# A decode block with attention and MLP: the pieces of w2's last row over six DMA engines, the bias loaded once, and o turned earlier on TensorE

## Chip, core and metric

The kernel runs on one core of a Trainium2 chip. The metric is device time in microseconds; 721.72 us is the median of three runs before the change (721.49 to 721.81). The profile is of one further execution.

## What is computed

For two sequences with one new token each (B = 2, D = 576), a sigmoid gate mixes an attention block and an MLP, all in float32:

```python
g = sigmoid((x * gate_w).sum(-1, keepdims=True))
# A: 32 heads, 4096 cached keys and values per head, head size 128
q = (x @ wq)                                  # 576 x 4096
scores = einsum("bhqd,bhkd->bhqk", q, k_cache) * 128 ** -0.5
o = einsum("bhqk,bhkd->bhqd", softmax(scores), v_cache)
a = o @ wo                                    # 4096 x 576
# B: hidden size 4608
b = gelu_tanh(x @ w1 + b1) @ w2 + b2          # 576 x 4608, then 4608 x 576
out = g * a + (1 - g) * b
```

The two caches hold 268 MB, the weights 40 MB; each byte is used once.

## The kernel before

**Loads.** All large loads are issued by SyncE (SP) into one ring in SBUF with three slots of 128 x 16384 floats. The order is fixed by a list: wq, w1, then K and V of sixteen groups of four heads in turn, then three "last" loads. A load is issued when the load three places ahead of it has been used up (`load_next`). `LAST` says what is in the last three: w2 rows 0-27 (in the layout `(p r) n`, each of the 128 partitions holds 36 rows of w2, and a "row" r in this text is the r-th row of every partition); then w2 rows 28-35 with `wx` and the first rows of wo (32 such rows); then the rest of wo in ever smaller transfers. The page's queue q1 carries these loads, q10 the small ones that ScalarE (ACT) issues.

**The pieces `wx`.** The last 288 columns of w2's row 35 are not in the main transfer (L158) but are loaded separately (L155): 128 runs of 288 floats, in four DMAs, to 16 partitions. The outer dimension of each of the four DMAs has XE = 4 entries, one to a DMA engine, with XS = 8 runs each. Since these rows then lie in other partitions than their multipliers, `hg[:, NF - 1]` is spread by small matmuls with slices of the identity into `hx` (L411, L415), and `mlp_x` multiplies `hx` with the pieces.

**Attention.** For each of the sixteen groups: VectorE multiplies K with the spread-out q (L506), VectorE and GpSimd sum over the head size (L510 to L512), the maximum and the exponentials follow (L516 to L531), and TensorE multiplies with V (`av`, L545). `keep` and `combine` gather the results in `oall`.

**The end.** `acc` in PSUM sums the MLP's output and wo's first rows (`acc_mm`, L367: each row is two halves of 288 columns, four matmul instructions). `mlp_out(lo, hi)` does rows of w2, `wo_out(0, FOLD)` rows 0 to 22 of wo, `last_out` copies `acc` to SBUF (L446), folds it into `res` (L467) together with wo's rows 23 to 31 (L457, L481), copies `res` out and stores it. Before wo, the attention result must be normalised (`norm_sum`), transposed (`norm_t`) and turned (`o_turn`) into the layout of wo's rows, `oP`. The order on TensorE is the order of the program's text: rows 0-13 of w2, the last `av`, rows 14-17, `combine`, the sums, rows 18-27, `norm_t`, `mlp_x`, `o_turn`, rows 28-35, wo.

**The bias.** b1 is loaded by ACT's queue for both sequences into `b1r`, once in one DMA (L218, at the start) and once in five, and is added to the hidden layer's sums (L390); L395 to L405 compute the gelu, `hg`. The second K load waits for `hg`.

Of the kernel before, what the change touches and what calls it, by code (L numbers as in the profile page):

```python
# [8 lines left out]
F32 = mybir.dt.float32  # L9
# [3 lines left out]
P = 128  # L13
# [6 lines left out]
def kernel(  # L20
# [14 lines left out]
    nc = tc.nc  # L35
    B, H, SK, DH = k_cache.shape
    D = x.shape[-1]
# [12 lines left out]
    NG = 4  # L50
# [3 lines left out]
    F4 = F // NG  # L54
    FR = F4 // P
    FB = 3
    FC = F4 // FB
    NF = F // P
    NC = 4
    DO = D // NC  # L60
    NS = 2
    DS = D // NS
# [2 lines left out]

    LAST = (
        (("w2", 0, 14), ("w2", 14, 28)),
        (("w2", 28, 36), ("wx", 0, 1), ("wo", 0, 8), ("wo", 8, 16)),
        (("wo", 16, 23), ("wo", 23, 27), ("wo", 27, 30), ("wo", 30, 31), ("wo", 31, 32)),
    )  # L70
    FOLD = 23
    SLOT = R * DH
# [8 lines left out]
    cp = ctx.enter_context(tc.tile_pool(name="cp", bufs=1))  # L81
# [8 lines left out]
    ps_sm = ctx.enter_context(tc.tile_pool(name="ps_sm", bufs=3, space=bass.MemoryType.PSUM))  # L90
# [8 lines left out]
    kt, vt, wqt, w1t, rows = {}, {}, {}, {}, {}  # L99
# [22 lines left out]
    def slot(n):  # L122
        k = len(held) % SLOTS
        return ring[:, k * SLOT:k * SLOT + n]
# [7 lines left out]

    srcs = {"w2": w2.rearrange("(p r) n -> p (r n)", r=NF), "wo": wo.rearrange("(p r) n -> p (r n)", r=32)}

    XE, XC = 4, 4
    XP = XE * XC
    XS = P // XP
    srcx2 = w2.rearrange("(e c s r) n -> c r e s n", e=XE, c=XC, s=XS)[:, NF - 1, :, :, DS:]

    def length(w, a, z):  # L140
        return XS * DS if w == "wx" else (z - a) * D - (DS if (w, z) == ("w2", NF) else 0)

    def load_last(m):
        n = sum(length(*q) for q in LAST[m])

        used["e"], used["z"] = len(held) % SLOTS * SLOT + n, (len(held) % SLOTS + 1) * SLOT
        t = slot(n)
        o = 0
        for w, a, z in LAST[m]:
            if w == "wx":  # L150
                xt = t[:XP, o:o + XS * DS]
                rows[w] = xt.rearrange("p (s n) -> p s n", s=XS)
                o += XS * DS
                for c in range(XC):
                    nc.sync.dma_start(xt[c::XC].rearrange("e (s n) -> e s n", s=XS), srcx2[c])  # L155
                continue
            if (w, z) == ("w2", NF):
                nc.sync.dma_start(t[:, o:o + length(w, a, z)], srcs[w][:, a * D:z * D - DS])  # L158
                for r in range(a, z):
                    rows[w, r] = t[:, o + (r - a) * D:o + min((r - a + 1) * D, length(w, a, z))]  # L160
                o += length(w, a, z)
                continue

            ends = (a * D, a * D + DS, a * D + DS + DO, z * D) if (w, z) == ("wo", 32) else (a * D, z * D)
            for u, v in zip(ends, ends[1:]):
                nc.sync.dma_start(t[:, o:o + v - u], srcs[w][:, u:v])
                o += v - u
            for r in range(a, z):
                rows[w, r] = t[:, o - (z - r) * D:o - (z - r - 1) * D]

    def temp(n, parts=P):
        t = ring[:parts, used["t"]:used["t"] + n]
        used["t"] += n
        assert used["t"] <= SLOTS * SLOT
        return t

    def late(n, parts=P):
        t = ring[:parts, used["e"]:used["e"] + n]
        used["e"] += n
        assert not seq and used["e"] <= used["z"]  # L180
        return t

    def load():
        if not seq:
            return
        kind, i = seq.pop()
        if kind == "wq":
            wqt[i] = load_w(wq, ROWS[kind], i)
        elif kind == "w1":
            w1t[i] = load_w(w1, ROWS[kind], i)  # L190
        elif kind == "k":
            kt[i] = load_heads(k_cache, i)
        elif kind == "v":
            vt[i] = load_heads(v_cache, i)
        else:
            load_last(i)
        if kind in ("k", "v", "last"):
            held.append((kind, i))
# [9 lines left out]
    b1r = temp(F4)  # L208
# [3 lines left out]
    load()  # L212
    load()

    def load_b1(b, ends):
        to, src = b1r.rearrange("(g q) n -> g q n", g=NG)[:, b], b1.rearrange("(g n) -> g n", g=NG)
        for u, v in zip(ends, ends[1:]):
            nc.scalar.dma_start(to[:, u:v], src[:, u:v])  # L218


    load_b1(0, (0, F4))
    for b in range(B):
        nc.scalar.dma_start(xg[b:b + 1], x[b])
    nc.scalar.dma_start(xg[B:B + 1], gate_w[None, :])
# [4 lines left out]
    ident = cp.tile([P, P], F32, name="ident")  # L229
# [9 lines left out]
    for j in range(NPB):  # L239
        t = cp.tile([P, NT * 32 + EB], F32, name=f"p{j}")  # L240
# [71 lines left out]
    for m, ps in enumerate(qps):  # L312
        nc.scalar.copy(qrow[:, m * 512:(m + 1) * 512], ps)
    nc.scalar.dma_start(b2r, b2[None, :])
    load_b1(1, (0, 232, 464, 696, 928, F4))

    to = temp(HG * NO).rearrange("p (f o) -> p f o", f=HG)
# [7 lines left out]
    for f in range(HG):  # L327
# [7 lines left out]
    row4 = temp(E, NO)  # L335
    nc.vector.tensor_reduce(row4, ident[:NO, :NO].rearrange("p (i e) -> p e i", e=E), AX.X, ALU.add)
    spread = cp.tile([NO, P], F32, name="spread")
    nc.vector.tensor_copy(
        spread.rearrange("p (e c) -> p e c", e=E), row4.unsqueeze(2).to_broadcast([NO, E, PE_])
    )  # L340
    qs = {}
# [19 lines left out]
    acc = ps_acc.tile([P, DS], F32, name="acc")  # L361

    def acc_mm(lhsT, rhs, k, start=False, stop=False, lo=0):
        m = lhsT.shape[-1]
        for s in range(lo, lo + rhs.shape[-1] // DS):
            o = 64 * (k % 2) + 32 * s
            nc.tensor.matmul(  # L367
                acc[o:o + m], lhsT, rhs[:, (s - lo) * DS:(s - lo + 1) * DS], start=start, stop=stop, skip_group_check=True
            )

    g1z = cp.tile([1, 2, 32], F32, name="g1z")
    nc.gpsimd.memset(g1z, 0.0)
# [1 line left out]
    for k in range(2):  # L374
        acc_mm(g1z[:, k], b2r, k, start=True)
# [17 lines left out]

    ht = temp(F4).rearrange("p (r c) -> p r c", c=32)
    nc.vector.transpose(ht, hrow.rearrange("q (p r) -> q r p", r=NF))  # L395
    hb = ht[:, :, :B]
    hg = cp.tile([P, NF, B], F32, name="hg")
    t = temp(NF * B).rearrange("p (r b) -> p r b", b=B)
    nc.vector.tensor_mul(t, hb, hb)
# [6 lines left out]

    load()

    hxps = ps_sm.tile([XP, XS, B], F32, tag="sm", name="hxps")
    for s in range(XS):  # L410
        nc.tensor.matmul(  # L411
            hxps[:, s], ident.rearrange("p (q s) -> p s q", s=XS)[:, s], hg[:, NF - 1], start=True, stop=True
        )
    hx = cp.tile([XP, XS, B], F32, name="hx")
    nc.scalar.copy(hx, hxps)  # L415

    def mlp_x():
        for s in range(XS):
            acc_mm(hx[:, s], rows["wx"][:, s], s, lo=1)

    def mlp_out(lo, hi):
        for r in range(lo, hi):
            acc_mm(hg[:, r], rows["w2", r], r)
# [4 lines left out]
    oP = cp.tile([P, B, 32], F32, name="oP")  # L428

    def o_turn(turn):  # L430
        t = late(B * 32).rearrange("p (b c) -> p b c", c=32)
        for b in range(B):
            nc.vector.transpose(t[:, b], oT[:, b])
        ps = ps_sm.tile([P, B * 32], F32, tag="sm", name="op_t")
        nc.tensor.matmul(ps, turn, t.rearrange("p b c -> p (b c)"), start=True, stop=True)
        nc.vector.tensor_copy(oP.rearrange("p b c -> p (b c)"), ps)

    def wo_out(lo, hi):
        for r in range(lo, hi):
            acc_mm(oP[:, :, r], rows["wo", r], r)  # L440
# [127 lines left out]
    def norm_sum():  # L568
        sums = ps_sm.tile([NO, 1], F32, tag="sm", name="psum")
        nc.tensor.matmul(sums, rs, ones, start=True, stop=True)  # L570
        f = late(1, NO)
        nc.vector.reciprocal(f, sums)
        nc.vector.tensor_mul(f, f, gall)
        nc.vector.tensor_reduce(osum, oall.rearrange("p (r d) -> p d r", d=DH), AX.X, ALU.add)
        nc.vector.tensor_scalar_mul(osum, osum, f[:, 0:1])

    def norm_t():
        ps = ps_sm.tile([P, NO], F32, tag="sm", name="oT_t")
        nc.tensor.transpose(ps, osum, ident[:NO, :NO])
        nc.vector.tensor_copy(  # L580
            oT.rearrange("p b (h e) -> p h b e", e=E), ps.rearrange("p (h b e) -> p h b e", b=B, e=E)
        )

# [29 lines left out]
    turn = late(P)  # L613
    nc.scalar.copy(turn.rearrange("p (h k) -> p k h", k=KB), ident.rearrange("p (k h) -> p k h", k=KB))
    osum = late(DH, NO)
    norm_sum()
    mlp_out(18, 28)
    norm_t()
    mlp_x()
    o_turn(turn)  # L620
    mlp_out(28, NF)
    wo_out(0, FOLD)
    last_out()

# [27 lines left out]
```

## Time and profile before

| | |
|---|---|
| runs | 721.49, 721.81, 721.72 us; median 721.72 |
| the profiled execution's own time | 721.61 us |
| its span, first to last instruction | 719.7 us |
| mean granted TensorE clock | 0.658 |
| busy: DVE / PE / POOL / PEld / ACT | 71 / 30 / 20 / 9 / 6% of the span |
| DMA | 308.85 MB, mean 429 GB/s; queue q1 99.2% of 16 engines' span |
| last stretch | 310 GB/s in the last fortieth of the span, 417 to 449 in most of the others |

Shares are of the span. "DMA share" is the mean busy share of the sixteen DMA engines; it can come out a little over 1 in a short stretch. The granted clock is 1.00 at full and 0.50 at half speed of TensorE. The timeline's rows are start, duration, engine, line, operation, operands and count; in brackets stands the idle time of the engine before them and what ended it.

### The profile page before, as it was taken

How to read it: one execution, taken by the hardware profiler on the slowest of the kernel's cores; microseconds unless marked ns; L12 is line 12 of the kernel's file. 1: busy time of each engine (PE TensorE's matmuls, PEld its weight loads, DVE VectorE, ACT ScalarE, POOL GpSimd, SP SyncE). 2: the span in 40 equal slices, each digit the busy share in tenths (PEclk: the TensorE clock that was granted, in tenths of full speed). 3: DMA queues.
4: the chain of work that ended last, by engine and by line, in shares of the span. 5: the costliest groups of instructions: out<-in, count | busy, mean ns of one | idle time of the engine just before them, and what ended most of it. 6: DMA issues, size and time to landing. Idle time of an engine off the chain costs nothing.

```text
span 719.7 us, 3881 instructions
## 1 busy us (share of the span) xinstructions
PE 216.2 (30%) x1647; PEld 62.6 (9%) x1647; DVE 511.8 (71%) x136; ACT 40.0 (6%) x156; POOL 145.0 (20%) x35
## 2 busy tenths in 40 slices
PE   0665022040515050404032140505050503113195
PEld 0322000010101010101000010101010100000032
DVE  0004969779695969596969879696959695988910
ACT  0110010100001010101010100001010101010000
POOL 2000130404050403022040404040503122040400
PEclk9977556575756575566657575657575665757599
DMA  9999999999999999999999999999999999999997
GB/s 409 412 446 427 423 452 415 459 416 452 423 437 424 444 426 430 442 430 441 433 431 437 430 426 444 427 437 437 437 427 448 419 434 433 430 441 434 417 424 310
DMA packets 7278, 308.85 MB, mean 429 GB/s; under 512 B 830, under 2 KB 1362, under 8 KB 1628
## 3 DMA queue, kind: packets, MB, share of 16 engines
q1 hardware_dynamic: 7204, 308.55, 99.2%
q8 instruction: 13, 0.21, 0.1%
q10 hardware_dynamic: 56, 0.05, 0.0%
q14 instruction: 5, 0.04, 0.0%
HBM read 308.59 MB, written 0.00 MB: 429 GB/s over the span
## 4 chain that ended last, share of the span: by engine, by line
DMA 47%; DVE 35%; PE 15%; ACT 1%; issue 1%; ACTq 1%; POOL 0%; DVEq 0%; SPq 0%; POOLq 0%
DMA ring<-in_A_k_cache_dram 38%; DVE ring L506 19%; DVE s L511 10%; PE av L545 10%; DVE s L512 5%; DMA ring<-in_B_w_dram 4%; DMA ring<-in_A_wo_dram 3%; DMA ring<-in_gate_w_dram 3%; PE oall L562 2%; PE qps L303 2%; PE acc L367 1%; DVE avs L556 1%; ACTq L218 0%; PE qps L328 0%; ACT p L531 0%
## 5 line engine op out<-in xcount | busy, mean ns | idle before, releaser
L506 DVE TENSOR_TENSOR ring<-ring,q 128x16384 f32<-128x16384 f32 x16 | 275.6, 17225 | 109.1 <-DMA ring<-in_A_k_cache_dram 109.1
L510 POOL TENSOR_TENSOR ring<-ring 128x3968 f32<-128x3968 f32 x16 | 137.0, 8565 | 490.1 <-DVE ring L506 490.1
L545 PE MATMUL av<-ring,p 128*32 128x512 f32 x1024 | 137.5, 698 | 166.9 <-ACT p L531 166.9
L511 DVE TENSOR_REDUCE s<-ring 128x66 f32<-128x8448 f32 x16 | 143.3, 8953 | 1.3
L562 PE MATMUL oall<-avs,pick 128*64 128x512 f32 x16 | 14.8, 1028 | 196.7 <-DVE avs L556 168.3
L512 DVE TENSOR_REDUCE s<-ring 128x62 f32<-128x3968 f32 x16 | 68.4, 4277 | 0.1
L545 PEld LDWEIGHTS av<-ring,p 128*32 128x32 f32 x1024 | 35.1, 127 | 274.8 <-issue 217.8
L531 ACT ACTIVATE p<-s,bs 32x128 f32<-32x128 f32 x64 | 25.5, 398 | 478.9 <-DVE bs L525 477.7
L351 PE MATMUL qb<-qm,spread 64*128 64x512 f32 x8 | 8.3, 1138 | 72.5 <-POOL qm L347 72.5
L390 DVE TENSOR_TENSOR ring<-hps,ring 128x384 f32<-128x384 f32 x3 | 1.7, 559 | 33.3 <-PE hps L303 33.1
L562 PEld LDWEIGHTS oall<-avs,pick 128*64 128x64 f32 x16 | 2.2, 196 | 203.5 <-DVE avs L556 203.5
L367 PE MATMUL acc<-ring,hg 128*2 128x288 f32 x142 | 11.9, 487 | 26.1 <-DMA ring<-in_B_w_dram 26.1
L283 DVE TENSOR_SCALAR gb<-gb 128x2 f32<-128x2 f32 x1 | 0.2, 170 | 24.7 <-ACT gb L282 24.7
L556 DVE TENSOR_TENSOR avs<-av,selr 128x512 f32<-128x512 f32 x8 | 5.5, 682 | 10.6 <-PE av L545 10.6
L303 PE MATMUL hps<-ring 128*32 128x384 f32 x120 | 12.8, 598 | 0.0
L347 POOL TENSOR_TENSOR qm<-qall,mine 64x512 f32<-64x512 f32 x4 | 4.1, 1032 | 41.7 <-ACT qall L330 41.7
L477 DVE COPY ring<-res 2x144 f32<-2x144 f32 x1 | 0.3, 297 | 16.4 <-PE res L457 16.4
L531 ACT ACTIVATION_READ_ACCUMULATOR p<-s,bs 32x1 f32 x64 | 11.8, 184 | 0.0
L303 PE MATMUL qps<-ring 128*32 128x512 f32 x80 | 11.3, 729 | 0.0
L270 PE MATMUL xps<-ident,ring 3*128 3x3 f32 x10 | 1.5, 254 | 24.0 <-DMA ring<-in_gate_w_dram 23.1
L351 PEld LDWEIGHTS qb<-qm,spread 64*128 64x128 f32 x8 | 2.0, 307 | 75.6 <-POOL qm L347 75.6
L353 ACT COPY q<-qb 128x512 f32<-128x512 f32 x4 | 2.3, 586 | 106.3 <-PE qb L351 106.3
(87 smaller groups left out, 74.3 us busy)
## 6 DMA issues: line engine op xcount, KB each, us to landing
ring<-in_B_w_dram SPq DMA_DIRECT2D x2, 4608.0 KB, 34.4
ring<-in_B_w_dram SPq DMA_DIRECT2D x2, 4032.0 KB
ring<-in_A_wo_dram SPq DMA_DIRECT2D x2, 2304.0 KB, 14.9
ring<-in_B_w_dram SPq DMA_DIRECT2D x1, 2160.0 KB
ring<-in_A_wo_dram SPq DMA_DIRECT2D x1, 2016.0 KB
ring<-in_B_w_dram SPq DMA_DIRECT2D x1, 1152.0 KB, 14.7
ring<-in_A_wo_dram SPq DMA_DIRECT2D x1, 1152.0 KB
ring<-in_A_wq_dram SPq DMA_DIRECT2D x1, 1024.0 KB
```

The source lines that it names most:

```text
L303: nc.tensor.matmul(ps[32 * j:32 * j + 32, :width], lhs, ts[c][:, o:o + width], start=(k == 0), stop=last, skip_group_check=True,)
L347: nc.gpsimd.tensor_mul(t, qall.unsqueeze(1).to_broadcast([NO, NQ, DH]), mine[:, u[0]:u[-1] + 1].unsqueeze(2).to_broadcast([NO, NQ, DH]),)
L351: nc.tensor.matmul(ps, spread, t.rearrange("p u d -> p (u d)"), start=True, stop=True)
L367: nc.tensor.matmul(acc[o:o + m], lhsT, rhs[:, (s - lo) * DS:(s - lo + 1) * DS], start=start, stop=stop, skip_group_check=True)
L506: nc.vector.tensor_mul(kt[i], kt[i], qs[i].unsqueeze(1).to_broadcast([P, R, DH]))
L510: nc.gpsimd.tensor_add(t[:, :, :DH2], t[:, :, :DH2], t[:, :, DH2:])
L511: nc.vector.tensor_reduce(st[i][:, HALVED:], kt[i][:, HALVED:], AX.X, ALU.add)
L512: nc.vector.tensor_reduce(st[i][:, :HALVED], t[:, :, :DH2], AX.X, ALU.add)
L531: nc.scalar.activation(p[w, :, e * RB:(e + 1) * RB], st[i][w].rearrange("p (t c) -> p t c", c=RB), AF.Exp, bias=bias[i][w], accum_out=rs[w ...
L545: nc.tensor.matmul(ps[32 * j:32 * j + 32], p[:, 32 * t + EB * (1 - half):32 * t + EB * (1 - half) + 32], vt[i][:, RB * t:RB * (t + 1)].rea ...
L556: nc.vector.tensor_mul(t, avs[i].rearrange("p (r d) -> p r d", d=DH), selr.unsqueeze(2).to_broadcast([P, RB, DH]))
L562: nc.tensor.matmul(oall, pick[:, NO - G - i * G:2 * NO - G - i * G], avs[i].rearrange("p r d -> p (r d)"), start=(i == 0), stop=(i == N // ...
```

## The change

- `wx` now holds the last 512 columns of row 35. Rows 0 to 119 of the 128 go in four DMAs with an outer dimension of XE = 6 and XS = 5 runs each (24 partitions), rows 120 to 127 in one more DMA with an outer dimension of 4 and 2 runs each. `hx` becomes two sets of multipliers (five and two). `acc_mm` cuts a range of columns at the border of the halves, so that each step of `mlp_x` is two matmuls, of 224 and 288 columns.
- wo's rows 0 to 14 are one transfer and rows 15 to 22 the next; before, they were 0-7, 8-15 and 16-22.
- On TensorE, `norm_t` and `o_turn` come after row 19 of w2; `mlp_x` and rows 20 to 35 follow.
- b1 is loaded once, in three pieces of 384 columns (one at the start, two later), to the row behind the two sequences' rows of each group; after the transpose one add on VectorE (`hb`) puts it to both sequences.
- Four small operations go from VectorE to ScalarE: the copy of `spread`, the scaling of `osum`, and the copies out of PSUM in `norm_t` and `o_turn`.

```diff
-        (("w2", 28, 36), ("wx", 0, 1), ("wo", 0, 8), ("wo", 8, 16)),
-        (("wo", 16, 23), ("wo", 23, 27), ("wo", 27, 30), ("wo", 30, 31), ("wo", 31, 32)),
+        (("w2", 28, 36), ("wx", 0, 1), ("wo", 0, 15)),
+        (("wo", 15, 23), ("wo", 23, 27), ("wo", 27, 30), ("wo", 30, 31), ("wo", 31, 32)),
...
-    XE, XC = 4, 4
+    XE, XC, XS, XW = 6, 4, 5, 512
     XP = XE * XC
-    XS = P // XP
-    srcx2 = w2.rearrange("(e c s r) n -> c r e s n", e=XE, c=XC, s=XS)[:, NF - 1, :, :, DS:]
+    XN = XP * XS
+    XR, XT = 4, (P - XN) // 4
+    XL = D - XW
+    srcw = w2.rearrange("(p r) n -> p r n", r=NF)[:, NF - 1, XL:]
+    srcx2 = srcw[:XN].rearrange("(e c s) n -> c e s n", e=XE, c=XC)
...
+                yt = t[:XR, o:o + XT * XW].rearrange("p (s n) -> p s n", s=XT)
+                nc.sync.dma_start(yt, srcw[XN:].rearrange("(p s) n -> p s n", s=XT))
...
-    load_b1(0, (0, F4))
+    def load_b1(lo, hi):
+        for m in range(lo, hi):
+            nc.scalar.dma_start(
+                b1r.rearrange("(g q) n -> g q n", g=NG)[:, B, m * FC:(m + 1) * FC],
+                b1.rearrange("(g n) -> g n", g=NG)[:, m * FC:(m + 1) * FC],
+            )
+
+    load_b1(0, 1)
...
-    load_b1(1, (0, 232, 464, 696, 928, F4))
+    load_b1(1, FB)
...
-    nc.vector.tensor_copy(
+    nc.scalar.copy(
         spread.rearrange("p (e c) -> p e c", e=E), row4.unsqueeze(2).to_broadcast([NO, E, PE_])
     )
...
-        for s in range(lo, lo + rhs.shape[-1] // DS):
+        hi = lo + rhs.shape[-1]
+        for s in range(NS):
             o = 64 * (k % 2) + 32 * s
+            u, v = max(lo, s * DS), min(hi, (s + 1) * DS)
+            if u < v:
+                nc.tensor.matmul(
+                    acc[o:o + m, u - s * DS:v - s * DS], lhsT, rhs[:, u - lo:v - lo],
+                    start=start, stop=stop, skip_group_check=True,
+                )
...
-    hb = ht[:, :, :B]
+    hb = temp(NF * B).rearrange("p (r b) -> p r b", b=B)
+    nc.vector.tensor_add(hb, ht[:, :, :B], ht[:, :, B:B + 1].to_broadcast([P, NF, B]))
...
+    hx = []
+    for n, lo, m in ((XP, 0, XS), (XR, XN, XT)):
+        ps = ps_sm.tile([n, m, B], F32, tag="sm", name=f"hxps{lo}")
+        to_x = ident[:, lo:lo + n * m].rearrange("p (q s) -> p s q", s=m)
+        for s in range(m):
+            nc.tensor.matmul(ps[:, s], to_x[:, s], hg[:, NF - 1], start=True, stop=True)
+        t = cp.tile([n, m, B], F32, name=f"hx{lo}")
+        nc.scalar.copy(t, ps)
+        hx += [t[:, s] for s in range(m)]
...
-        nc.vector.tensor_copy(oP.rearrange("p b c -> p (b c)"), ps)
+        nc.scalar.copy(oP.rearrange("p b c -> p (b c)"), ps)
...
-        nc.vector.tensor_scalar_mul(osum, osum, f[:, 0:1])
+        nc.scalar.mul(osum, osum, f[:, 0:1])
...
-        nc.vector.tensor_copy(
+        nc.scalar.copy(
             oT.rearrange("p b (h e) -> p h b e", e=E), ps.rearrange("p (h b e) -> p h b e", b=B, e=E)
         )
...
-    mlp_out(18, 28)
+    mlp_out(18, 20)
     norm_t()
+    o_turn(turn)
     mlp_x()
-    o_turn(turn)
-    mlp_out(28, NF)
+    mlp_out(20, NF)
     wo_out(0, FOLD)
     last_out()
```

More of the change, by code (lines that the diff above doesn't have):

```diff
@@ L133 @@
     srcs = {"w2": w2.rearrange("(p r) n -> p (r n)", r=NF), "wo": wo.rearrange("(p r) n -> p (r n)", r=32)}
-    XE, XC = 4, 4
+    XE, XC, XS, XW = 6, 4, 5, 512
     XP = XE * XC
-    XS = P // XP
-    srcx2 = w2.rearrange("(e c s r) n -> c r e s n", e=XE, c=XC, s=XS)[:, NF - 1, :, :, DS:]
+    XN = XP * XS
[3 more added lines that the diff above has]
+    srcx2 = srcw[:XN].rearrange("(e c s) n -> c e s n", e=XE, c=XC)
     def length(w, a, z):
-        return XS * DS if w == "wx" else (z - a) * D - (DS if (w, z) == ("w2", NF) else 0)
+        return (XS + XT) * XW if w == "wx" else (z - a) * D - (XW if (w, z) == ("w2", NF) else 0)
     def load_last(m):
@@ L146, in load_last @@
         used["e"], used["z"] = len(held) % SLOTS * SLOT + n, (len(held) % SLOTS + 1) * SLOT
+        assert n <= SLOT
         t = slot(n)
@@ L150, in load_last @@
             if w == "wx":
-                xt = t[:XP, o:o + XS * DS]
-                rows[w] = xt.rearrange("p (s n) -> p s n", s=XS)
-                o += XS * DS
+                xt = t[:XP, o:o + XS * XW]
                 for c in range(XC):
                     nc.sync.dma_start(xt[c::XC].rearrange("e (s n) -> e s n", s=XS), srcx2[c])
+                o += XS * XW
+                yt = t[:XR, o:o + XT * XW].rearrange("p (s n) -> p s n", s=XT)
+                nc.sync.dma_start(yt, srcw[XN:].rearrange("(p s) n -> p s n", s=XT))
+                o += XT * XW
+                xt = xt.rearrange("p (s n) -> p s n", s=XS)
+                rows[w] = [xt[:, s] for s in range(XS)] + [yt[:, s] for s in range(XT)]
                 continue
             if (w, z) == ("w2", NF):
-                nc.sync.dma_start(t[:, o:o + length(w, a, z)], srcs[w][:, a * D:z * D - DS])
+                nc.sync.dma_start(t[:, o:o + length(w, a, z)], srcs[w][:, a * D:z * D - XW])
                 for r in range(a, z):
@@ L213 @@
     load()
[L215 to L218, printed above, removed]
-    load_b1(0, (0, F4))
+    def load_b1(lo, hi):
[5 more added lines that the diff above has]
+    load_b1(0, 1)
     for b in range(B):
@@ L364, in acc_mm @@
         m = lhsT.shape[-1]
-        for s in range(lo, lo + rhs.shape[-1] // DS):
+        hi = lo + rhs.shape[-1]
+        for s in range(NS):
             o = 64 * (k % 2) + 32 * s
-            nc.tensor.matmul(
-                acc[o:o + m], lhsT, rhs[:, (s - lo) * DS:(s - lo + 1) * DS], start=start, stop=stop, skip_group_check=True
-            )
+            u, v = max(lo, s * DS), min(hi, (s + 1) * DS)
[4 more added lines that the diff above has]
+                )
     g1z = cp.tile([1, 2, 32], F32, name="g1z")
@@ L407 @@
     load()
[L409 to L415, printed above, removed]
+    hx = []
[7 more added lines that the diff above has]
+        hx += [t[:, s] for s in range(m)]
     def mlp_x():
-        for s in range(XS):
-            acc_mm(hx[:, s], rows["wx"][:, s], s, lo=1)
+        for s in range(XS + XT):
+            acc_mm(hx[s], rows["wx"][s], s, lo=XL)
     def mlp_out(lo, hi):
```

## The prediction

> **What bounds the kernel now.** I read the page first (shares and queues), then busy time by stage, then the last stage in steps of half a microsecond, the chain of waits, and the timelines of TensorE and of the queues around the edits.
>
> ```profile
> span 719.7 us, 3881 instructions
> PE 216.2 (30%) x1647; PEld 62.6 (9%) x1647; DVE 511.8 (71%) x136; ACT 40.0 (6%) x156; POOL 145.0 (20%) x35
> ...
> q1 hardware_dynamic: 7204, 308.55, 99.2%
> q8 instruction: 13, 0.21, 0.1%
> q10 hardware_dynamic: 56, 0.05, 0.0%
> ```
> ```profile
> 5.00:100.00 95.00, 34.67 (x262) 14.43 (x262) 36.33 (x23) 5.52 (x21) 9.68 (x3) 0.76 1.01 436
> 300.00:400.00 100.00, 27.48 (x184) 6.69 (x176) 83.28 (x15) 4.50 (x17) 21.37 (x4) 0.64 1.00 435
> 690.00:700.00 10.00, 10.00 (x111) 3.35 (x103) 2.41 (x8) 0.43 (x1) 0.00 (x0) 1.00 1.01 429
> 700.00:712.00 12.00, 7.79 (x120) 3.00 (x122) 0.22 (x1) 0.00 (x0) 0.00 (x0) 1.00 0.99 422
> ```
>
> In these stage rows the columns are busy time of PE, PEld, DVE, ACT, POOL, then granted clock, DMA share, GB/s. No compute engine is full. The DMA engines are: q1 alone takes 99.2% of sixteen engines' span, and the share is 0.99 to 1.01 in every stage down to 712 us. One engine moves 435 / 16 = 27.2 KB per us. With no gap in the stream, a load issued earlier buys nothing; only the bytes that the most burdened engine moves, and what follows its last byte, set the end.
>
> ```profile
> 713.50:714.00 0.50, 0.50 (x24) 0.44 (x20) 0.00 (x0) 0.00 (x0) 0.00 (x0) 1.00 0.95 374
> 714.00:714.50 0.50, 0.50 (x24) 0.35 (x16) 0.00 (x0) 0.00 (x0) 0.00 (x0) 1.00 0.78 303
> 714.50:715.00 0.50, 0.22 (x8) 0.00 (x0) 0.00 (x0) 0.00 (x0) 0.00 (x0) 1.00 0.59 214
> 715.00:715.50 0.50, 0.14 (x8) 0.13 (x11) 0.00 (x0) 0.00 (x0) 0.00 (x0) 1.00 0.52 194
> 715.50:716.00 0.50, 0.50 (x24) 0.40 (x16) 0.00 (x0) 0.00 (x0) 0.00 (x0) 1.00 0.46 158
> 716.00:716.50 0.50, 0.50 (x22) 0.17 (x12) 0.00 (x0) 0.00 (x0) 0.00 (x0) 1.00 0.47 119
> 716.50:717.00 0.50, 0.50 (x15) 0.24 (x12) 0.10 (x1) 0.06 (x1) 0.00 (x0) 1.00 0.00 0
> ```
> ```profile
> 695.27 20.04 DMA ring<-in_A_wo_dram
> 715.31 0.04 issue
> 715.36 1.56 PE res L457 x36
> ```
>
> The engines do not end together. From 713.5 to 716.5 the share falls from 0.95 to 0.47: about a third of them are done by 714.7, half by 715.5, and the last at 716.5. The unused part is 0.5 x (0.05+0.22+0.41+0.48+0.54+0.53) = 1.1 us per engine. So with the same bytes, no redistribution can end the transfers more than 1.1 us earlier; that caps the gain. The chain confirms it: the end waits for wo, then 1.6 us of TensorE; a copy and the store follow.
>
> **The change, part by part.**
>
> *Row 35.* The main transfer of w2 rows 28-35 loses 512 - 288 = 224 columns, 896 B in each partition; with 8 partitions to an engine that is 7,168 B, **-0.26 us on all sixteen engines**. The pieces now hold 128 runs of 1,152 B on engines 0 to 3: 36,864 B each, 1.36 us. After, 120 runs of 2,048 B lie on engines 0 to 5 (20 each, 40,960 B), and the remaining 8 on engines 0 to 3 (2 each, 4,096 B). Net by engine: 0 to 3, 45,056 - 36,864 - 7,168 = +1,024 B, +0.04 us; **4 and 5, +33,792 B, +1.24 us**; 6 to 15, -0.26 us. The runs also have a price of their own. While they pass (690-700) the cores moved 429 GB/s against 435: 60 KB missing in 10 us, at 27.2 KB per us 2.2 engine-us over 128 runs, at most 17 ns a run. Engines 0 to 3 have 22 runs for 32, so up to -0.17 us; engines 4 and 5 up to +0.34 us.
>
> The Trainium skill, DMA: Bandwidth & Descriptors, section Bandwidth, speaks against the pieces: transfers under 64 KB are dominated by descriptors, with 0.95 us listed for 64 KB. By that figure the four pieces of 60 KB and the small one would cost an estimated 4.5 us on engines 4 and 5 instead of my 1.5. The trace disagrees already for the four pieces of 36 KB: the share stays 1.01 in the stretch in which they pass.
>
> Which engines end last? No view names them. If 4 and 5 are among those done by 715.0, they end at 716.2 to 716.6 and the rest decide: -0.13 to -0.26 us. If they are among the last, the end moves by +1.24 to +1.58 us. I take the first. The packet records behind the page, read one after another, join into sixteen sequences: the instruction blocks of q8 go in turn to half of them, the 1,152 B runs mark engines 0 to 3 among the others, and the four sequences left over, with neither, end first. That their numbers are 4 to 7 is my inference, and so it stays a matter of chance.
>
> *wo in one transfer, split at 15.* The bytes and their order stay, one issue goes and one (the small piece of w2) comes. The cost lies on TensorE:
>
> ```profile
> 701.90 2.34 PE L367 MATMUL acc<-ring,oP 128*2 128x288 f32 x31
> 705.82 2.12 PE L367 MATMUL acc<-ring,oP 128*2 128x288 f32 x32 [1.58 <-DMA ring<-in_A_wo_dram]
> 710.57 2.11 PE L367 MATMUL acc<-ring,oP 128*2 128x288 f32 x28 [2.63 <-DMA ring<-in_A_wo_dram]
> 713.31 1.16 PE L457 MATMUL res<-ring,oP 128*2 128x144 f32 x32 [0.63 <-DMA ring<-in_A_wo_dram]
> 716.67 0.48 PE L481 MATMUL res<-ring,oP 128*2 128x72 f32 x8
> ```
>
> Rows 0-7 no longer run at 701.9 but wait for rows 0-14. Those land one row earlier than rows 8-15 do now (18,432 B per engine, 0.68 us) and 0.26 us lower, about 704.9. They are 60 matmuls at 2.12 / 32 = 66 ns, 4.0 us, to 708.9, still ahead of 710.57. The next batch has 32 for 28: +0.27 us, against an idle 0.63 us ahead of 713.31. Nothing reaches the end: **0**, covered by waits for wo that stay.
>
> *o turned earlier.*
>
> ```profile
> 695.42 0.68 DVE L574 TENSOR_REDUCE ring<-oall 64x128 f32<-64x512 f32 x1
> 696.14 0.28 DVE L575 TENSOR_SCALAR ring<-ring 64x128 f32<-64x128 f32 x1
> 697.58 0.27 PE L579 MATMUL oT_t<-ident,ring 64*128 64x64 f32 x1
> 697.79 2.10 PE L367 MATMUL acc<-ring,hx 16*2 16x288 f32 x16
> 697.89 0.23 DVE L580 COPY oT<-oT_t 128x64 f32<-128x64 f32 x1 [1.48 <-PE oT_t L579]
> 698.15 0.31 DVE L433 STREAM_TRANSPOSE ring<-oT 128x32 f32<-128x32 f32 x2
> 699.82 0.43 PE L435 MATMUL op_t<-ring 128*128 128x64 f32 x2
> ```
>
> Now 40 matmuls and the pieces cover this chain. After, only rows 18 and 19 do (8 matmuls, to about 695.6). TensorE then waits: until the scaling, on ACT now, ends at about 696.5, and from 696.8 to about 697.6 for the copy and the transposes. Two waits, 0.9 + 0.8 = 1.7 us; everything on PE (pieces, rows 20-35, wo) queues behind them. The small operations that go from DVE to ACT take 0.23 and 0.28 us on DVE now; ACT is 6% busy, and were each twice as long there, the waits would grow by 0.5 us, still covered. The pieces become 28 matmuls for 16: 1.9 us at 66 ns, 3.4 us at most (2.10 / 16 = 131 ns). Rows 20-35 follow, 62 matmuls, 4.1 us: done at 703.6 to 705.1, where wo lands at 704.9. **0**, with the idle 1.58 us ahead of 705.82 as cover; if it runs over, the 1.7 us up to 710.57 takes it.
>
> *Bias and hb.*
>
> ```profile
> 39.79 2.65 ACTq L218 DMA_DIRECT2D ring<-in_B_b_dram  x5
> ...
> 68.47 0.23 DVE L405 TENSOR_TENSOR hg<-ring,g 128x72 f32<-128x72 f32 x1
> 68.91 0.33 SPq L130 DMA_DIRECT2D ring<-in_A_k_cache_dram  x1
> ```
>
> b1 is loaded once: 18,432 B less, on the four engines that one row per engine uses, 4,608 B, **-0.17 us on engines 0 to 3**. Three DMA issues fewer leave ACT 1.6 us earlier. The added add of 128x72 costs DVE 0.23 us and puts the second K load's issue from 68.91 to 69.2; the stream is at 1.01 there, so it queues behind work: 0.
>
> *TensorE's instructions.* Pieces +24, turns of hx -4: 20 of 3,294, some 1.3 KB of the 0.21 MB of q8. Between 0 and one further 16 KB block, 0.6 us, on one engine: 0 taken.
>
> **Sum.** Engines 6 to 15 -0.26 us; engines 0 to 3 +0.04 - 0.17 = -0.13, with fewer runs down to -0.30. The later of them decides: I take **-0.2 us**. The profiled execution took 721.61 us for a span of 719.7; that gives 721.4. The median, 721.72, lies 0.11 above it; I forecast **721.5 us** for the median. No difference under 0.2% (1.44 us) can be told from no change here.
>
> **Rivals.**
> 1. *Engines 4 and 5 are among the last.* For it: 8 engines are still busy at 715.5, none named. Against: the packet sequences. +1.24 to +1.58 us: 722.9 to 723.3, on the edge of what can be told.
> 2. *Slower: the clock halves in the last stage.* Rows of 3.4 us show how the clock goes:
>
> ```profile
> 111.80:115.20 3.40, 1.24 (x12) 0.12 (x4) 3.40 (x1) 0.00 (x0) 0.00 (x0) 1.00 1.07 463
> 115.20:118.60 3.40, 0.00 (x0) 0.00 (x0) 3.40 (x1) 0.00 (x0) 0.00 (x0) 0.50 0.80 347
> 613.50:616.90 3.40, 1.61 (x16) 0.27 (x8) 3.40 (x1) 0.00 (x0) 0.00 (x0) 1.00 0.93 405
> 616.90:620.30 3.40, 0.00 (x0) 0.00 (x0) 3.40 (x1) 0.00 (x0) 0.00 (x0) 1.00 0.98 424
> ```
> TensorE busy for 1.24 of 3.4 us (0.36) was followed by 0.50; 1.61 (0.47) was not. The new waits leave 3.4 - 1.7 = 1.7 us (0.50), just above. The Trainium skill, TensorE: Matmul & The Clock Gate, Part 1, asks for a whole idle window of 3.4 us before the clock falls; by it nothing would happen here, but the first row fell at 0.36 busy. If the waits reach 2.2 us, one window runs at half speed and some 1.7 us of work slips, into the 1.6 and 1.7 us of waits: under 0.3 us. It decides only if a window under 0.4 lies behind 709, so that the last 1.56 and 0.48 us double: +2.0 us, 723.6. Against it: the longest wait there, 2.63 us now, shrinks to about 1.5.
> 3. *The pieces fall on fewer engines than six, or cost by the piece.* On three, 81,920 B each, 3.0 us for 1.36: 723.0; on two, 122,880 B, 724.5. Against: now four groups pass at an undiminished share.
> 4. *Faster:* the late engines happen to be relieved more; the cap is 1.1 us, 720.5, inside 0.2%.
>
> **How the numbers follow.** Forecast 0.80; rival 1 0.10, a third of it over the edge; rival 2 0.03; rival 3 0.04; rival 4 0.03. Faster by over 0.2% needs more than the cap; I count rival 4 for it whole, 0.03, since the cap rests on one execution. Slower: a third of rival 1, rival 2 and half of rival 3, 0.03 + 0.03 + 0.02 = 0.08. Same: the rest, 0.89. The forecast alone spans 721.1 (-0.3, and the median's 0.11 either way) to 721.9; the range reaches to the gain of 1.1 us in part and to the lower end of rival 1: 720.9 to 722.9.
>
> **What would show it.** DMA share 1.00 down to 712 and falling later and steeper than now, zero from about 716.3; TensorE idle for about 0.9 and 0.8 us around 696-697.6; one wait for wo ahead of 15 rows near 704.9; no idle of 2.6 us ahead of rows 15-22; granted clock 1.00 to 719. Wrong: a share near 0.12 (two engines) for a microsecond at the end means rival 1 or 3; a clock of 0.50 before 717 means rival 2.

## Result and profile after

The changed kernel takes 723.05 us (median of 17 runs, 722.36 to 724.79); the kernel before took 721.57 us beside it (17 runs, 721.41 to 722.33). The ratio is 1.0022, with a 95% interval of 1.0016 to 1.0029: slower by about 1.5 us. The profiled execution took 722.94 us, 1.33 us more than that of before.

The head of the page, rows of the same kind as those shown of before:

```profile
span 721.0 us, 3897 instructions
...
PE 221.1 (31%) x1657; PEld 65.1 (9%) x1657; DVE 510.9 (71%) x133; ACT 41.1 (6%) x161; POOL 145.0 (20%) x35
...
q1 hardware_dynamic: 7072, 308.55, 99.1%
q8 instruction: 13, 0.21, 0.1%
q10 hardware_dynamic: 32, 0.03, 0.0%
```

The busy times hardly moved, and the transfers still fill the span. The span grew by 1.3 us. Its end, first in the chain of waits and then in half-microsecond windows (columns as before):

```profile
696.04 20.45 DMA ring<-in_A_wo_dram
716.49 0.04 issue
716.53 1.49 PE res L474 x36
```
```profile
715.50:716.00 0.50, 0.36 (x12) 0.04 (x4) 0.00 (x0) 0.00 (x0) 0.00 (x0) 1.00 0.79 294
716.00:716.50 0.50, 0.00 (x0) 0.00 (x0) 0.00 (x0) 0.00 (x0) 0.00 (x0) 1.00 0.61 210
716.50:717.00 0.50, 0.47 (x16) 0.42 (x20) 0.00 (x0) 0.00 (x0) 0.00 (x0) 1.00 0.52 158
717.00:717.50 0.50, 0.50 (x24) 0.26 (x14) 0.00 (x0) 0.00 (x0) 0.00 (x0) 1.00 0.07 22
```

The chain has the same links as before: a wait for wo, about 1.5 us of TensorE, a copy, the store. But the wait ends at 716.49, not at 715.31: 1.18 us later, nearly all of the 1.3 us. The DMA share has the shape that it had, about a microsecond later: 0.46 at 715.5 to 716.0 before, 0.52 at 716.5 to 717.0 now. Two engines left alone would show a share near 0.12 for a microsecond; instead the whole set is late, and only after 717.0 is one engine left alone, at a share of 0.07. So the loss lies in the stream, the loads that run one behind the other through the DMA queue, ahead of the last stage. One finds where by following VectorE's multiplications of K, which begin, but for the first, when K has landed. The timeline of VectorE, before:

```profile
70.36 17.22 DVE L506 TENSOR_TENSOR ring<-ring,q 128x16384 f32<-128x16384 f32 x1 [1.17 <-DMA ring<-in_A_k_cache_dram]
108.96 17.23 DVE L506 TENSOR_TENSOR ring<-ring,q 128x16384 f32<-128x16384 f32 x1 [7.41 <-DMA ring<-in_A_k_cache_dram]
147.63 17.23 DVE L506 TENSOR_TENSOR ring<-ring,q 128x16384 f32<-128x16384 f32 x1 [7.48 <-DMA ring<-in_A_k_cache_dram]
```

and after:

```profile
74.54 17.21 DVE L523 TENSOR_TENSOR ring<-ring,q 128x16384 f32<-128x16384 f32 x1
109.53 17.23 DVE L523 TENSOR_TENSOR ring<-ring,q 128x16384 f32<-128x16384 f32 x1 [3.82 <-DMA ring<-in_A_k_cache_dram]
148.68 17.23 DVE L523 TENSOR_TENSOR ring<-ring,q 128x16384 f32<-128x16384 f32 x1 [7.95 <-DMA ring<-in_A_k_cache_dram]
```

The first multiplication begins 4.18 us later and no longer waits for K: K is there, the program is late. The second, which waits for K again, is 0.57 us later, the third 1.05 us. These starts alone don't say how much the stream lost, since each waits for the engine that lands last: the lag is 0.88 us at the fourth multiplication, 2.36 at the seventh and 0.96 at the last two. (Each of the two executions has one interval between two multiplications that is over 1.3 us longer than its neighbours, ahead of the seventh here and ahead of the fifteenth before; its cause was not looked for.) The bytes say it. The table sums the DMA packets of the traces, each spread evenly over its own time, and gives in us, at 435 GB/s, by how much a kernel's stream is ahead of that of before (+) or behind it (-); the last three kernels are those of the first three experiments below.

| up to | 66 us | 75 us | 100 us | 120 us | 700 us |
|---|---|---|---|---|---|
| changed kernel | +0.03 | -0.41 | -0.46 | -1.02 | -1.02 |
| its later bias pieces behind the copies | +0.04 | +0.06 | +0.06 | +0.06 | +0.08 |
| the bias alone | +0.13 | -0.84 | -0.84 | -0.88 | -0.86 |
| the bias alone, its later pieces late | +0.06 | +0.08 | +0.08 | +0.04 | -0.25 |

The changed kernel's stream lost 1.0 us between 66 and 120 us and nothing after it. What made the program late is in ScalarE's timeline and in the queue of SyncE, which issues the loads. Before, then after, of ScalarE:

```profile
42.49 0.89 ACT L322 COPY ring<-ident 128x8 f32<-128x8 f32 x8 [2.36 <-issue]
```
```profile
40.09 1.05 ACTq L226 DMA_DIRECT2D ring<-in_B_b_dram  x2
48.02 0.90 ACT L332 COPY ring<-ident 128x8 f32<-128x8 f32 x8 [7.60 <-DMA ring<-in_B_b_dram]
```

and of SyncE, before and then after:

```profile
45.75 0.33 SPq L130 DMA_DIRECT2D ring<-in_A_k_cache_dram  x1
61.43 0.33 SPq L130 DMA_DIRECT2D ring<-in_A_v_cache_dram  x1
```
```profile
38.11 0.33 SPq L130 DMA_DIRECT2D ring<-in_A_k_cache_dram  x1
66.57 0.33 SPq L130 DMA_DIRECT2D ring<-in_A_v_cache_dram  x1
74.31 0.33 SPq L130 DMA_DIRECT2D ring<-in_A_k_cache_dram  x1
```

After its two issues for b1, ScalarE stands for 7.60 us until those bytes have landed, and only then copies the identity into `to`, eight small copies that have nothing to do with the bias. Before, the five issues cost it 2.65 us, and then the copies ran at once. Behind the copies stand q's products with `to`, then w1's products, the hidden layer, the gelu. Four links of the chain of waits of the changed kernel:

```profile
40.64 7.28 DMA ring<-in_B_b_dram
48.02 0.21 ACT ring L332
48.28 3.69 PE qps L338 x16
57.45 11.74 PE hps L313 x120
```

w1's slot comes free only after w1's products, so the first V load is issued at 66.57 for 61.43, and the second K load, which waits for the gelu, at 74.31 for 68.91: both more than 5 us late. The first K load, on the other hand, is issued 7.6 us earlier, and that bought nothing.

### The profile page after: what moved, and what is told of

The parts are those of the page before. It is cut to its first block, busy times and chain, and to the rows that moved or that the text cites. A ratio compares the mean times of both kernels' runs of the same rounds, so it can differ in the third digit from the quotient of the medians.

```text
span 721.0 us, 3897 instructions
## 1 busy us (share of the span) xinstructions
PE 221.1 (31%) x1657; PEld 65.1 (9%) x1657; DVE 510.9 (71%) x133; ACT 41.1 (6%) x161; POOL 145.0 (20%) x35
## 4 chain that ended last, share of the span: by engine, by line
DMA 44%; DVE 36%; PE 18%; ACT 1%; issue 1%; ACTq 0%; POOL 0%; DVEq 0%; POOLq 0%
DMA ring<-in_A_k_cache_dram 34%; DVE ring L523 19%; DVE s L528 10%; PE av L562 10%; DVE s L529 5%; DMA ring<-in_B_w_dram 4%; DMA ring<-in_A_wo_dram 3%; DMA ring<-in_gate_w_dram 3%; PE oall L579 2%; PE hps L313 2%; PE qps L313 2%; PE acc L380 1%; DMA ring<-in_B_b_dram 1%; PE qps L338 1%; DVE avs L573 1%
## 5 line engine op out<-in xcount | busy, mean ns | idle before, releaser
L562 PE MATMUL av<-ring,p 128*32 128x512 f32 x1024 | 139.4, 706 | 160.2 <-ACT p L548 160.2
L380 PE MATMUL acc<-ring,hg 128*2 128x288 f32 (+1 forms) x142 | 14.2, 562 | 26.0 <-DMA ring<-in_B_w_dram 26.0
```

Of the source, the lines that this page charges most:

```text
L380: nc.tensor.matmul(acc[o:o + m, u - s * DS:v - s * DS], lhsT, rhs[:, u - lo:v - lo], start=start, stop=stop, skip_group_check=True,)
L562: nc.tensor.matmul(ps[32 * j:32 * j + 32], p[:, 32 * t + EB * (1 - half):32 * t + EB * (1 - half) + 32], vt[i][:, RB * t:RB * (t + 1)].rea ...
```

## Theories and experiments

The theory to be tested: the wait of ScalarE for the later b1 pieces delays the first V load and the second K load so far that the stream runs dry for a moment; that is the whole loss. It is theory A of the expectations. Its rivals: the pieces of row 35 make engines 4 and 5 the last; or the clock of TensorE halves in the last stage.

### The later bias pieces issued behind the copies

```diff
-    load_b1(1, FB)
...
     for f in range(HG):
         nc.scalar.copy(to[:, f]..., ident...)
+    load_b1(1, FB)
```

> The changed kernel, with the two later pieces of the bias issued behind ScalarE's eight copies into `to` instead of ahead of them, so that the first copy no longer waits 7.6 us for the second piece to land. Theory A (that wait delays q, the w1 products, the first V load by 5 us and, by way of the gelu, the second V load; the DMA stream runs dry twice and stands 1.0 us later from then on): first V load issued by 62 us, second K load by 70, DMA share without a hole at 68 and 107, the K load after it landed at 146.2 on average instead of 147.3; time 1.0 us below the changed kernel, 721.8 to 722.1. Theory B (the pieces on engines 4 and 5, or engines 0 to 3, set the end): hole gone or not, time stays at 722.8 to 723.2.

Measured: 721.63 us (721.33 to 722.98, 11 runs) against 721.59, ratio 1.0005 (0.9996 to 1.0014). ScalarE, SyncE and the third multiplication in its timelines:

```profile
39.25 0.90 ACT L331 COPY ring<-ident 128x8 f32<-128x8 f32 x8
```
```profile
55.08 0.33 SPq L130 DMA_DIRECT2D ring<-in_A_v_cache_dram  x1
```
```profile
147.49 17.23 DVE L523 TENSOR_TENSOR ring<-ring,q 128x16384 f32<-128x16384 f32 x1 [7.29 <-DMA ring<-in_A_k_cache_dram]
```

The copies do not wait; the V load goes out at 55.08, and the third multiplication begins at 147.49 (147.63 before). Moving one line gives back the microsecond and a half in seven of eleven runs (721.33 to 721.66); the other four lie at 722.79 to 722.98, a second group to which the last experiments return. The expected hole in the DMA share can't be read in steps of 2 us, which in every one of these kernels swing between about 0.4 and 1.4; the table of bytes shows it. A load that is 6 us earlier than before brings nothing beyond that: this stream gained nothing from an early issue and lost when one came too late.

### The change of the bias alone

Before, with the new `load_b1` and the add `hb`, all else as it was.

> The kernel before, with the change's bias alone (three pieces, one row per group, one add after the transpose). Theory A: slower than before by the whole hole, 0.9 to 1.2 us: 722.5 to 722.8; DMA share with holes at 68 and 107. Theory B: as before, 721.4 to 721.7 (4.6 KB less on four engines).

Measured: 723.07 us (722.51 to 724.09, 11 runs), ratio 1.002 (1.0012 to 1.0029): the whole loss, without pieces, without wo in one transfer, without the new order.

```profile
47.76 0.89 ACT L323 COPY ring<-ident 128x8 f32<-128x8 f32 x8 [7.94 <-DMA ring<-in_B_b_dram]
```
```profile
65.95 0.33 SPq L130 DMA_DIRECT2D ring<-in_A_v_cache_dram  x1
```
```profile
149.41 17.23 DVE L508 TENSOR_TENSOR ring<-ring,q 128x16384 f32<-128x16384 f32 x1 [8.83 <-DMA ring<-in_A_k_cache_dram]
```

The same wait, the same late V load, and the third multiplication 1.78 us later than before. Some 1.3 us of that is the one long interval, which this execution has ahead of its third multiplication; at the sixteenth the lag is 0.50 us, and the bytes are 0.86 us behind. Its end is later than that: from 717.0 to 718.5 the share is still 0.13 to 0.17, which is two engines alone, and the last transfer ends at 718.3 instead of 716.5. Why these two fall behind by more than the whole set was not settled; what the traces of this kernel and of the changed one show for the stream as a whole is 0.9 to 1.0 us.

### The bias alone, with its later pieces behind the copies

The same kernel with `load_b1(1, FB)` moved as in the first experiment. This separates the wait from what else the bias's change does (one row fewer, three pieces, the add).

> The kernel before with the change's bias alone, its two later pieces issued behind ScalarE's copies into `to`. Theory A (the bias costs 1.5 us only through the wait ahead of these copies): back to the kernel before, 721.3 to 721.7, against 723.07 of the bias alone; first V load by 62 us. Rival H (the added add on VectorE or the renumbered DMA semaphores cost it): 722.5 and up. For the upper group at +1.2 us that the kernels with the new pieces show in some runs: if the pieces cause it, no run here above 722.2; if the bias does, some.

Measured: 721.92 us (721.67 to 722.10, 11 runs), ratio 1.0004 (0.9995 to 1.0013); the kernel with the wait was 1.15 us above it, and no run of the one reaches the other.

```profile
38.56 0.90 ACT L322 COPY ring<-ident 128x8 f32<-128x8 f32 x8
```
```profile
147.28 17.23 DVE L508 TENSOR_TENSOR ring<-ring,q 128x16384 f32<-128x16384 f32 x1 [7.33 <-DMA ring<-in_A_k_cache_dram]
```

The wait is the cause; what the rest of the bias's change does can't be told from nothing. That the copies wait for the transfer at all is the program's doing, not the data's: they neither read b1 nor write its columns of the ring. In the kernel before, the view of waits names the same tensor as what SyncE's first K load waited for, 9.3 us up to 45.75, and that load had time to spare: its earlier issue bought nothing. Why the new pieces make the copies wait where the former ones didn't was not settled.

### The order on TensorE and wo in one transfer, alone

Before, with wo's rows 0-14 in one transfer, `norm_t` and `o_turn` after row 19, and the four small operations on ScalarE.

> The kernel before, with wo's rows 0 to 14 in one transfer, o turned after row 19, and the four operations on ScalarE; bias and pieces as before. Theory A: TensorE's new waits and a half clock from about 699 are covered by waits for wo: no difference, 721.4 to 721.8. Theory C (the clock falls to a half behind the new waits, and the products of wo then end later than the last transfers): 722.3 and up, no idle time of TensorE ahead of the last products.

Measured: 721.54 us (721.41 to 721.78, 11 runs), ratio 0.9999 (0.9990 to 1.0008). Nothing, as forecast.

### Everything but the pieces, the bias late

> The changed kernel with the bias issued late and the pieces as before (288 columns over four engines). If the new pieces cause the upper group: one group, 721.3 to 721.8. If the earlier turn of o causes it: some runs at 722.5 and up, as in the late-bias kernel.

The kernel just named (order and wo) with the bias as in the kernel before that, its later pieces behind the copies: 721.77 us (721.58 to 722.08, 11 runs), ratio 1.0002 (0.9993 to 1.0011). Nothing, and one group of times.

### The pieces alone

Before, with `wx` of 512 columns over six engines; wo is cut at 8, 15, 23, so that it fits the slot.

> The kernel before, with the 512 columns of row 35 in pieces over engines 0 to 5 alone (and wo split at row 15 instead of 16, so that it fits the slot). Theory A: the pieces are worth what the bytes say, -0.3 to +0.2 us: 721.3 to 721.8. Theory B: engines 4 and 5 or 0 to 3 end last, +1.2 us or more: 722.8 and up, last landing 1.2 us later than before.

Measured: median 722.54 us (721.38 to 722.98, 11 runs), ratio 1.0008 (0.9999 to 1.0017), but in two groups: four runs at 721.38 to 721.58, seven at 722.54 to 722.98. Its profile fell into the upper one (722.54). First windows of 3.4 us, then TensorE's timeline:

```profile
705.90:709.30 3.40, 1.28 (x20) 0.29 (x9) 0.00 (x0) 0.00 (x0) 0.00 (x0) 1.00 0.98 420
709.30:712.70 3.40, 2.23 (x20) 0.70 (x24) 0.00 (x0) 0.00 (x0) 0.00 (x0) 0.51 0.97 407
712.70:716.20 3.50, 3.50 (x52) 1.64 (x48) 0.00 (x0) 0.40 (x1) 0.00 (x0) 0.50 0.76 285
```
```profile
710.47 4.02 PE L377 MATMUL acc<-ring,oP 128*2 128x288 f32 x32 [3.29 <-DMA ring<-in_A_wo_dram]
714.26 2.09 PE L470 MATMUL res<-ring,oP 128*2 128x144 f32 x32
```

Here the transfers are not late (the share is 0.00 from 716.4 on). TensorE is: after a window with 1.28 of 3.4 us busy its clock stood at 0.50 from 709.3 to 716.2. The 32 products took 4.02 us where 28 took 2.11, the next 32 took 2.09 instead of 1.16, and the two waits of 0.6 us that could have absorbed it are gone. A further profile of the same kernel, of an execution of 721.40 us, has the granted clock at 1.00 throughout this stage; the same 32 products:

```profile
710.37 2.12 PE L377 MATMUL acc<-ring,oP 128*2 128x288 f32 x32 [3.32 <-DMA ring<-in_A_wo_dram]
```

> The kernel with the pieces alone, one look. If above 722.3: theory M (half clock in the last stage), last landing near 716.7, clock 0.50 behind the wait of 3.3 us, store issued 1.8 us behind the last landing; theory E (an engine with pieces ends late), last landing 717.5 or later and the store 0.8 us behind it. Below 721.8 both have clock 1.00 or a short half window and a landing at 716.7.

> The same once more: above 722.3, theory M has the last landing near 716.7 and the store 1.8 us behind it, theory E the last landing at 717.5 or later and the store 0.8 us behind it.

In the expectations theory M is the half clock in the last stage, theory E an engine with pieces that ends late. The other profile, of 721.64 us, lies between: the same wait of 3.31 us, then a fall at 711.3 when the products already run, 3.31 us for the 32, and the clock back at 714.8. So one kernel, in this stage, has executions with none, one and two windows at half clock; of these three, only the one with two lies in the upper group.

### wo cut at 15 alone

Is the longer wait ahead of the 32 products (3.29 us for 2.63) enough for the upper group?

```diff
-        (("w2", 28, 36), ("wx", 0, 1), ("wo", 0, 8), ("wo", 8, 16)),
-        (("wo", 16, 23), ("wo", 23, 27), ...
+        (("w2", 28, 36), ("wx", 0, 1), ("wo", 0, 8), ("wo", 8, 15)),
+        (("wo", 15, 23), ("wo", 23, 27), ...
```

> The kernel before with wo cut at row 15 instead of 16 (rows 0-7, 8-14, 15-22) and nothing else. The kernel with the pieces alone, which has this cut too, ran in two groups, four runs at 721.4 to 721.6 and seven at 722.5 to 723.0; its profile shows the clock at 0.50 from 709.3 after a wait of 3.3 us, and 32 products in 4.0 us. Theory M: the longer wait ahead of rows 15 to 22 does it, not the pieces: two groups here too, with at least a third of the runs at 722.3 to 723.0. Rival P (the pieces do it): all runs at 721.4 to 721.8.

Measured: 721.63 us (721.42 to 721.77; one further run of 889 us is left out of the ratio), ratio 1.0000 (0.9991 to 1.0009): one group. In its profile the clock falls too, but later:

```profile
707.90:711.30 3.40, 0.72 (x12) 0.32 (x16) 0.00 (x0) 0.00 (x0) 0.00 (x0) 0.99 1.00 426
711.30:714.70 3.40, 3.40 (x41) 1.47 (x37) 0.00 (x0) 0.40 (x1) 0.00 (x0) 0.50 0.93 379
```
```profile
710.58 3.41 PE L367 MATMUL acc<-ring,oP 128*2 128x288 f32 x32 [3.29 <-DMA ring<-in_A_wo_dram]
```

The fall comes when the products already run; the next window is busy throughout, and the clock is back at 714.7. The products took 3.41 us, and the execution 721.62: one half-clock window is absorbed by the idle time ahead of the last batches. Where the fall comes before the products, as in the first profile of the pieces, the window after it is still partly idle, a second one at half clock follows, and that reaches the end. The Trainium skill, TensorE: Matmul & The Clock Gate, Part 1, calls the window free-running, not reset by the kernel; two executions of one kernel that differ so agree with it. It asks for a whole idle window of about 3.4 us before the clock falls; here windows with 1.28 and 0.72 us of work were enough, so the measured rows decide.

### The pieces' products last, the bias late

If a thin stretch ahead of wo starts the upper group, filling another one should remove it: `mlp_x` behind `mlp_out(20, NF)`, in the kernel of the first experiment.

> The changed kernel with the bias issued late, as before, and the products with the pieces moved behind rows 20 to 35 of w2. The late-bias kernel ran in two groups, seven runs at 721.3 to 721.7 and four at 722.8 to 723.0. Theory M (in the upper group TensorE stays at half clock for one window of 3.4 us more, because the products with the pieces, 24 rows deep, directly follow the waits and do not count as full activity; the sums of wo then end 1.2 us too late): with full products behind the waits the clock is back after at most two windows, and all runs lie at 721.3 to 721.8. Rival S (the upper group comes from the start of the kernel, where the first V load is late in some runs): a third of the runs at 722.8 and up as now.

Measured: 721.91 us (721.37 to 723.44, 11 runs), ratio 1.0008 (0.9999 to 1.0017); six runs to 721.91, five from 722.45. The groups stayed; the expectation failed. Two more profiled executions, 721.44 and 721.50 us, and four of the first experiment's kernel, 721.52, 721.53, 721.41 and 721.75 us, were all of the lower group and so could not show what the upper one is in these two kernels. (Rival S of the expectations is a first V load that is late in some runs.)

> The kernel with the pieces' products last and the bias late once more, one look, for a profile of its upper group (5 of 11 runs at 722.4 to 723.4). If above 722.3: theory E (an engine with pieces ends late) shows a last landing of wo at 717.5 or later with one or two engines apart from the rest; theory M (half clock in the last stage) shows it near 716.6, and TensorE busy without a break up to the end. Below 721.8 it says nothing.

> The same as the look before, for a second chance: theory E, a late last landing where the time is above 722.3; theory M, a last landing near 716.6 and half clock.

> The late-bias kernel once more, one look, for a profile of its upper group. Theory M: if the time is above 722.5, the granted clock is 0.50 for three windows (10 us) from about 697 and TensorE has no idle time ahead of the last products of wo; if it is below 721.8, for two windows. Rival S: above 722.5 the first V load is issued after 64 us and the DMA share has a hole near 68.

> The same as the look before, for a second chance at the upper group: Theory M, three windows of half clock where the time is above 722.5; Rival S, a late first V load there.

> The late-bias kernel, one look. Above 722.3: theory M, three windows of half clock from about 697 and the products of wo late, last landing near 716.5; theory E, last landing at 717.5 or later. Below 721.8: two windows, landing near 716.5.

> The same once more: above 722.3, theory M has three windows of half clock and a last landing near 716.5, theory E a last landing at 717.5 or later.

### Four engines, and 288 columns

Two versions of the kernel with the pieces alone: `XE, XC, XS, XW = 4, 4, 8, 512` without a remainder (wo cut at 8, 14, 23), and `6, 4, 5, 288`.

> As the kernel with the pieces alone (512 columns, bias and order as before), but the pieces on engines 0 to 3 only: 32 runs of 2,048 B each, 65,536 B for the 36,864 B of before, less 7,168 B: +21,504 B, +0.79 us on engines 0 to 3 and -0.26 us on the others; wo is cut at 8, 14, 23. Theory of the engines (the group 1.2 us higher comes from engines 4 and 5 being last in some executions): no group near 722.7; either all near 721.6 (0 to 3 have slack) or all near 722.1 to 722.4 (they have none). Theory of the products (512 columns, two products for a step, let the clock fall late in some executions): two groups again, 721.4 to 721.7 and 722.5 to 723.0, some half of the runs in the upper.

> As the kernel with the pieces alone, but with 288 columns as before on engines 0 to 5: 20 runs of 1,152 B, 23,040 B, new on engines 4 and 5 (+0.85 us), 25,344 B for 36,864 B on 0 to 3 (-0.42 us), one product for a step as before (14 for 16). Theory of the engines: two groups, the upper one nearer, 0.8 to 0.9 us above the lower (721.5 and 722.3). Theory of the products: one group, 721.4 to 721.8, as before.

Measured: on four engines 723.58 us (722.45 to 724.13, 11 runs), ratio 1.0025 (1.0016 to 1.0034); three runs lie at 722.45 to 722.53, eight from 723.08. With 288 columns 722.39 us (721.49 to 723.27, 11 runs), ratio 1.0012 (1.0003 to 1.0021), spread over the whole stretch. Neither theory's pattern came out: the upper times don't need engines 4 and 5, and they don't need 512 columns. The profile of the one with 288 columns (722.85 us) again has two half-clock windows; its full clock is given as 0.95 all through, so it is not quite like the others:

```profile
706.30:709.70 3.40, 1.02 (x16) 0.20 (x4) 0.00 (x0) 0.00 (x0) 0.00 (x0) 0.93 0.93 396
709.70:713.10 3.40, 2.51 (x24) 0.87 (x28) 0.00 (x0) 0.00 (x0) 0.00 (x0) 0.50 1.00 418
713.10:716.40 3.30, 3.30 (x52) 1.61 (x45) 0.00 (x0) 0.40 (x1) 0.00 (x0) 0.50 0.65 244
```
```profile
710.59 4.02 PE L377 MATMUL acc<-ring,oP 128*2 128x288 f32 x32 [3.27 <-DMA ring<-in_A_wo_dram]
```

The other profile (722.52 us) has one half-clock window and transfers that go on to about 717.2 instead of 716.5: close to the 0.79 us that its bytes on engines 0 to 3 had been priced at. So these engines seem to have no slack of that size; which of the two set the time was not separated.

What stays open: why kernels with the new pieces have upper times (16 of the 33 timed runs of the three that share 512 columns on six engines) and those without have not (none of 44: the bias alone and late, the order alone, all but the pieces, wo cut at 15 alone; its run of 889 us apart). Two halved windows in the last stage are seen in two profiles of upper runs, and in none of the lower ones that late. That they make the upper group of the late-bias kernel and of the one with the pieces' products last is not shown: no upper run of these two was profiled, and rival 1, engines 4 and 5 as the last at +1.24 us, would give a gap of much the same size there.

## Why the prediction was wrong

The forecast was 721.5 us in a range of 720.9 to 722.9; measured, 723.05. By its steps:

- **The step that failed is the bias, priced at 0.** It said "Three DMA issues fewer leave ACT 1.6 us earlier" and of the second K load's issue, taken to move from 68.91 to 69.2, that "it queues behind work: 0". The load moved to 74.31, the V load ahead of it by 5.14 us, and the cost was 1.2 to 1.5 us (the bias alone, 723.07 for 721.59; its wait, 1.15). The working counted issues, bytes and the added add. It didn't ask whether what follows on ScalarE waits for the new transfers: b1's later pieces had become a release for the copies into `to`. The row `42.49 ... [2.36 <-issue]` would have been the place to look: the copies then waited for nothing but ScalarE's own queue, so a new wait there had no cover, and behind it stands the chain to the V load.
- **The bound by the stream was right, its corollary too wide.** "A load issued earlier buys nothing" holds (V at 55.08 brought nothing). That a later one costs nothing holds only while the queue has work: 5 us exceeded the cover, and the stream came out 0.9 to 1.0 us behind.
- **The bytes of row 35 were not contradicted, and no more than that.** With the wait removed, the lower group (721.33 to 721.66) stands some 0.3 us under the kernel with everything but the pieces (721.58 to 722.08); -0.26 was the price. But the lower group is a choice among the runs, and a difference of that size can't be told from nothing here. Rival 1 is in none of the profiles of kernels with the new pieces on six engines; their upper runs were profiled once with 512 columns and once with 288. Its sign, a share near 0.12 for a microsecond, did appear, in the bias alone, which has no new pieces: so the sign doesn't single rival 1 out. Rival 3, the pieces on fewer engines than six, didn't occur: the late-bias profile of 721.33 us would have shown its 1.5 us or more. The 4.5 us worked out from the Trainium skill's figure (DMA: Bandwidth & Descriptors, section Bandwidth) did not show either: in the packet records a run of 1,152 B took 0.051 us before and one of 2,048 B takes 0.084 us now, so the 22 runs on one engine make 1.85 us, where the 32 of before made 1.63.
- **wo and o at 0: right.** The timeline of TensorE in the changed kernel:

```profile
697.25 0.27 PE L596 MATMUL oT_t<-ident,ring 64*128 64x64 f32 x1 [0.87 <-ACT ring L592]
698.16 0.43 PE L452 MATMUL op_t<-ring 128*128 128x64 f32 x2 [0.64 <-DVE ring L450]
698.52 3.08 PE L380 MATMUL acc<-ring,hx 24*2 24x224 f32 x28
707.55 6.26 PE L380 MATMUL acc<-ring,oP 128*2 128x288 f32 x90
714.45 1.16 PE L474 MATMUL res<-ring,oP 128*2 128x144 f32 x32 [0.65 <-DMA ring<-in_A_wo_dram]
```

The two new waits are 0.87 and 0.64 us (0.9 and 0.8 forecast). But rows 20-35 ended at 707.5, not by 705.1, and the single wait for wo near 704.9 was not there: wo's rows followed without a break to 713.8. An idle 0.65 us remained ahead of 714.45, so the cover held, by less than thought.

- **The clock was misread, without cost here.** The windows of that stretch:

```profile
696.10:699.50 3.40, 1.88 (x31) 1.10 (x26) 0.96 (x4) 1.20 (x4) 0.00 (x0) 1.00 1.01 437
699.50:702.90 3.40, 3.40 (x26) 0.91 (x22) 0.00 (x0) 0.00 (x0) 0.00 (x0) 0.50 0.95 410
702.90:706.30 3.40, 3.40 (x34) 1.05 (x29) 0.00 (x0) 0.00 (x0) 0.00 (x0) 0.50 0.93 398
```

The forecast set the threshold between 0.36 and 0.47 and put this window at 0.50, "just above". It had 0.55 busy, and the clock fell. That was rival 2's first half, and it cost nothing, as that rival said of a fall in this place: the order alone has the same fall, from 699.3 to 706.2 in its profile, and took 721.54 us. Its second half, a fall that lasts into the last products, is what the profile of the pieces alone shows; rival 2 had priced it at +2.0 us, and the two profiles with it stood 1.0 and 1.3 us above the median of before.

## To carry to other kernels

When a change alters a DMA, list not only its bytes and issues but every instruction that will now wait for its landing; a small load that nothing reads until 20 us after it has landed stalled the engine that starts a long chain. In this kernel, whose DMA stream is full, an issue 6 us early was worth nothing, and one 5 us late cost about 1 us, so the issue times of the loads, compared between the two traces, are the first thing to read. To see how much a full stream lost, add up the bytes: the start of what waits for a load follows the engine that lands last. And ask of each long wait ahead of the end not only how long it is but whether the batch behind it could run at half clock.

## What the runs showed of the hardware

A fixed share of busy time doesn't tell when the clock falls: it fell after windows with 0.72, 1.02, 1.28 and 1.88 of 3.4 us busy, while 1.61 had kept it in the trace of before; the windows were placed by the changes of the granted clock and the stretches before them. It could also stay at 0.50 through a window that was busy throughout (699.5 to 702.9, mostly products of 24 rows), while after the fall at 711.3 one busy window, of full products, brought it back. And a load issued 5 us late near the start was seen 580 us later in the bytes: the stream was 1.02 us behind at 120 us and 1.02 at 700, and nothing in the groups between made it up.
